# Low halves of two blocks moved to GpSimd, and the weight conversions placed one f later, in a gated linear attention and feed-forward kernel

## The chip, the cores and the metric

The kernel runs on one core of a Trainium2 chip. Its engines have instruction streams of their own: TensorE (PE in the profile; PEld is its weight load), VectorE (DVE), ScalarE (ACT), GpSimd (POOL) and SyncE (SP), which issues the transfers here. The metric is the device time of one execution in microseconds.

## What is computed

A gated linear attention over 4 batches, 8 heads, 768 steps and a head dimension of 48, whose output goes as 3072 tokens of 384 through a feed-forward layer of width 2048 with a leaky ReLU:

```python
for t in range(S):
    state = alpha[:, :, t, :, None] * state + np.einsum('bhd,bhe->bhde', k[:, :, t], v[:, :, t])
    y[:, :, t] = np.einsum('bhd,bhde->bhe', q[:, :, t], state)
x = y.transpose(0, 2, 1, 3).reshape(B * S, H * D)
h = x @ w_in
g = np.maximum(0.01 * h, h)
out = g @ w_out
```

q, k, v and alpha are float32. The two weight matrices are float64 and come to the kernel as pairs of 32-bit words.

## The kernel before

**Attention.** The work is cut into 24 units (a chunk of 128 tokens of one batch, all heads). The generator `attention` issues a unit in steps: `scans`, `scores`, `mask_scores` (a copy on ScalarE, L353, and a mask on GpSimd, L354), `k_tokens`, `scaled_q`, `scaled_k`, `outputs` (which writes x as a high half on ScalarE, L404, and a low half on VectorE, L405) and `next_state` (with a scaling on GpSimd, L359). Three units make a block `i` of 384 tokens, so there are eight blocks. Units 0 to 8 run first and give blocks 0, 1 and 2.

**Feed-forward.** An item is a pair (i, f): block i and one of 16 slices f of the width. `ffn_in` multiplies x by the weights of f. To keep precision, each operand is split into a high and a low half, and three products are summed: nine matmuls of 384 columns into one of two `ph` buffers (L473). Then L476 (ScalarE) makes `t` = 0.01 ph, L479 (VectorE) the maximum of it and ph, L481 (ScalarE) the high half `gh` and L485 (VectorE) the low half `gl`. `ffn_out` adds another nine matmuls (L498) per item into the output sums, `LAG` = 3 items later in program order. The items of blocks 0 and 1 alternate over f: (0,0), (1,0), (0,1), (1,1) and so on. The other blocks follow one by one, with the attention of the units 9 to 23 between their items. The first eight attention steps of that part are each held behind the low half (`made["gl", ...]`) of the item in front.

**Weights.** `load_weights(f)` brings slice f of both matrices into one of four `raw` buffers through SP's queue. When the last slice has been asked for, the loads of the units 9 and up follow behind it. `converting(f)` is a generator that turns the 64-bit words into a high and a low float32 half. It yields behind each of its eight steps: L233 (ScalarE, scales the upper words in place), L235 and L238 (VectorE, the float32 bits), L241 (ScalarE, the high half), L245 (VectorE, a power of two), L247 (VectorE, bits minus high half), L249 (VectorE, the lower words; the last reader of `raw`), L252 (VectorE, the low half).

**The order.** The framework's scheduler orders each engine's instructions, within edges that the kernel sets. `put(True, engine, op)` ties each instruction behind the last one that was put on the same engine's list, so that these lists are executed in program order:

```python
line = lines[eng]
with tc.issue_after(line[-1].ins) if line else nullcontext():
    line.append(op(*args))
```

`ffn_in` takes two tuples of generators and advances each one step per mention: the first tuple between L476 and L479, the second between L481 and L485. In the main loop `new` and `coming` are conversions on their way. Before the change, the conversions of f = 0 and f = 1 (`EARLY` = 2) are issued during the attention of the units 7 and 8, that of f = 2 as a whole behind x of unit 8, and from then on the conversion of f + 3 begins in item (0, f), while that of f + 2 is carried on and ends in the next f's first item. So one conversion overlaps the next, and is complete a whole f before its use. With the tuples of before, VectorE's list for one f reads L479, L235, L252, L238, L485 in item (0, f), and L245, L479, L247, L485, L249 in item (1, f), where L252 belongs to the older conversion.

Of the kernel before, what the change touches and what calls it, by code (L numbers as in the profile page):

```python
# [9 lines left out]
F32 = mybir.dt.float32  # L10
# [5 lines left out]
ALU = mybir.AluOpType  # L16
# [6 lines left out]
def gated_linear_attn_ffn(ctx, tc, q, k, v, alpha, w_in, w_out, out):  # L23
    nc = tc.nc
# [32 lines left out]
    PITCH = RUN + GAP  # L57
    AHEAD = 3 * UPB
    LAG = 3
    SOON, EARLY = 2, 2  # L60
    LEAD = 8
    SL = 8 * UPB

# [32 lines left out]
    def w_in_of(f, n, g):  # L96
        return w_sb[f][:, n, g * P:(g + 1) * P]
# [4 lines left out]
    made = {}  # L102
# [3 lines left out]
    def behind(*key):  # L106

        return tc.issue_after(made[key].ins) if key in made else nullcontext()
# [31 lines left out]
    def load_values(u):  # L140
        if u >= NU:
            return
        if u >= AHEAD and later is not None:
            later.append((load_values, u))
            return
        tb, b = units[u]
        made["v", u] = nc.sync.dma_start(
            vals_sb[u % NV].rearrange("t (h d) -> t h d", h=H),
            v[b, :, tb * C:(tb + 1) * C, :].rearrange("h t d -> t h d"),
        )  # L150
# [38 lines left out]
    def load_weights(f, part=None):  # L189

        if part != 1:
            jobs[f] = cvp.tile([P, 2 * NG, 2 * P], I32, name="raw", bufs=NRAW)
        raw = jobs[f]
        dst = raw.bitcast(I64) if f64 else raw[:, :, 0:P].bitcast(F32)
        for r, n, src, step, group in runs if part != 0 else ():
            a = w_in[src:src + n, f * P:(f + 1) * P]
            nc.sync.dma_start(  # L197
                dst[r:r + n, 0:NG], bass.AP(a.tensor, a.offset, [[step * DF, n], [group * DF, NG], list(a.ap[1])])
            )
        if part != 1:  # L200
            made["raw", f] = nc.sync.dma_start(dst[:, NG:], w_out[f * P:(f + 1) * P, :].rearrange("p (g f) -> p g f", g=NG))
# [3 lines left out]
    def put(ordered, eng, op, *args):  # L205

        if not ordered:
            return op(*args)
# [3 lines that stand above are left out]
        return line[-1]  # L212

    def converting(f, ordered=False):

        if f >= NF:
            return
        raw = jobs.pop(f)
        w_sb[f] = cst.tile([P, 2, 2 * DM], F32R, name=f"w{f}")
        hi, lo = w_sb[f][:, HIGH, :], w_sb[f][:, LOW, :]  # L220
        if not f64:
            val = raw[:, :, 0:P].bitcast(F32)
            hi, lo = (t.rearrange("p (g f) -> p g f", f=P) for t in (hi, lo))
            nc.scalar.copy(hi, val)
            made["w", f] = nc.vector.tensor_tensor(lo, val, hi.bitcast(F32), ALU.subtract)
            return
        words = raw.rearrange("p g (f w) -> p (g f) w", w=2)
        top, low = words[:, :, 1], words[:, :, 0]
        bits = cvp.tile([P, 2 * DM], I32, name="bits", bufs=NBITS)
        val = bits.bitcast(F32)  # L230

        with nullcontext() if lines["ACT"] else behind("hi", f - 1):
            put(ordered, "ACT", lambda: nc.scalar.mul(top.bitcast(F32), top.bitcast(F32), 2.0 ** -112))  # L233
        yield
        put(ordered, "DVE", lambda: nc.vector.tensor_scalar(  # L235
            bits, top, 3, 0x7FFFFFF8, ALU.logical_shift_left, ALU.bitwise_and))
        yield
        put(ordered, "DVE", lambda: nc.vector.scalar_tensor_tensor(  # L238
            bits, top, -0x80000000, bits, ALU.bitwise_and, ALU.bitwise_or))
        yield  # L240
        made["hi", f] = put(ordered, "ACT", lambda: nc.scalar.copy(hi, val))  # L241
        yield
        pw = cvp.tile([P, 2 * DM], I32, name="pw", bufs=NPW)
        rest = pw.bitcast(F32)
        put(ordered, "DVE", lambda: nc.vector.tensor_scalar(pw, bits, -0x800000, None, ALU.bitwise_and))  # L245
        yield
        put(ordered, "DVE", lambda: nc.vector.tensor_tensor(val, val, hi.bitcast(F32), ALU.subtract))  # L247
        yield
        put(ordered, "DVE", lambda: nc.vector.scalar_tensor_tensor(  # L249
            rest, low.bitcast(U32), 2.0 ** -52, rest, ALU.mult, ALU.mult))  # L250
        yield
        made["w", f] = put(ordered, "DVE", lambda: nc.vector.tensor_tensor(lo, rest, val, ALU.add))  # L252

    def convert(f):
        for _ in converting(f):
            pass
# [207 lines left out]
    def ffn_in(i, f, steps=None):  # L464

        ordered = steps is not None
        first, second = steps or ((), ())
        xh, xl = xs[i]
        ph = ps_h.tile([P, 512], F32, name="ph")[:, 0:TB]
        n = 0  # L470
        for g in range(NG):
            for wn, xt in ((HIGH, xh), (HIGH, xl), (LOW, xh)):
                nc.tensor.matmul(ph, w_in_of(f, wn, g), xt[:, g, :], start=n == 0, stop=n == 3 * NG - 1)  # L473
                n += 1
        t = ffp.tile([P, TB], F32, name="t")
        put(ordered, "ACT", lambda: nc.scalar.mul(t, ph, 0.01))  # L476
        for step in first:
            next(step, None)
        put(ordered, "DVE", lambda: nc.vector.tensor_tensor(t, ph, t, ALU.max))  # L479
        gh = ffp.tile([P, TB], F32R, name="gh", bufs=LAG + 1)  # L480
        put(ordered, "ACT", lambda: nc.scalar.copy(gh, t))  # L481
        for step in second:
            next(step, None)
        gl = ffp.tile([P, TB], F32R, name="gl", bufs=LAG + 1)
        made["gl", i, f] = put(ordered, "DVE", lambda: nc.vector.tensor_tensor(gl, t, gh.bitcast(F32), ALU.subtract))  # L485
        return gh, gl

    pos = {}
# [28 lines left out]
    gs = {}  # L517
# [8 lines left out]
    for n, _ in enumerate(st):  # L526
        if n == 2:
            load_values(NV - 1)
        while LOADS and LOADS[0][0] in made:
            key, f, part = LOADS.pop(0)  # L530
            with behind(*key):
                load_weights(f, part)
            loaded_f = f + 1
        u = AHEAD - EARLY + converted
        if converted < EARLY and ("ks", u) in made:
            with behind("ks", u):
                convert(converted)
            converted += 1
        if n in STARTS:
            i, f = items[len(gs)][:2]  # L540
            with behind(*STARTS[n]):
                gs[len(gs)] = ffn_in(i, f)
# [7 lines left out]
    new, coming = None, converting(EARLY + 1, True)  # L550
    next(coming)
    for n in range(len(items) + LAG):
        slices = 0
        if n < len(items):
            i, f, slices, _ = items[n]
            if f == 0:
                if i == 2:
                    st, held = attention(AHEAD, NU), 8
                while i not in ready:
                    next(st)  # L560
                emitted, due = 0, 0.0
            if loaded_f < NF:
                load_weights(loaded_f)
                loaded_f += 1
                if loaded_f == NF:
                    asked, later = later, None
                    with behind("raw", NF - 1):
                        for fn, *args in asked:
                            fn(*args)
            if n < len(STARTS):  # L570
                pass
            elif i == 0:
                old, new, coming = new or iter(()), coming, converting(f + SOON + 1, True)
                gs[n] = ffn_in(i, f, ((), (coming, new, old, new)))
            elif i == 1:
                gs[n] = ffn_in(i, f, ((new, new), (new,)))
                next(new, None)
            else:
                gs[n] = ffn_in(i, f)
        for half in range(2):  # L580
            due += slices / 2
            while emitted < due:

                with behind("gl", *items[n - 1][:2]) if held else nullcontext():
                    next(st, None)
                held = max(held - 1, 0)
                emitted += 1
            if half == 0 and n >= LAG:
                i, f, _, tag = items[n - LAG]
                ffn_out(i, f, gs.pop(n - LAG), tag)  # L590
# [129 lines left out]
```

## Time and the profile before

| what | value |
|---|---|
| median of 3 runs | 542.4 us (541.23 to 542.99) |
| profiled execution, first to last instruction (span) | 539.2 us |
| mean granted TensorE clock | 0.994 |
| L473, matmuls of `ffn_in` | 1152 of 338 ns mean |
| L479 and L485 on VectorE | 128 each of 550 ns mean |
| L476 and L481 on ScalarE | 128 each of 489 and 513 ns mean |
| a conversion's steps on VectorE (L235, L238, L245, L247, L249, L252) | 561, 950, 564, 969, 948, 970 ns mean |
| a conversion's steps on ScalarE (L233, L241) | 915, 838 ns mean |

The page names no total of the profiled execution but its span. Matmuls overlap, so their mean duration is longer than the distance from one to the next. Neighbouring VectorE instructions overlap too by some 0.08 us, so sums are made from starts and not from durations. In a row of the timeline stand start, duration, engine, line and operation, then what is written from what; in brackets the idle time in front of it and what ended it.

### The profile page before, as it was taken

The numbers are of one execution on the slowest core, as the hardware profiler recorded it, in microseconds if no ns is written. First come the engines' busy times: TensorE is split into PE (matmuls) and PEld (weight loads), VectorE is DVE, ScalarE is ACT, GpSimd is POOL, SyncE is SP. The second block draws the span as 40 slices with busy tenths as digits, with TensorE's granted clock in tenths as the row PEclk, the third lists the DMA queues.
The fourth block names the chain that finished last, engine by engine and source line by source line (L and its number), as shares of the span: only waits on it lengthen the run. The fifth ranks groups of instructions, "written<-read, shape, count | busy, mean of one in ns | idle before, by whom it ended". The sixth has DMA issues, their size and how long they took to land.

```text
span 539.2 us, 10037 instructions
## 1 busy us (share of the span) xinstructions
PE 522.2 (97%) x3778; PEld 501.8 (93%) x3778; DVE 380.5 (71%) x695; ACT 233.7 (43%) x494; POOL 60.2 (11%) x139
## 2 busy tenths in 40 slices
PE   8889889999999999999999999999999999999995
PEld 8778689999999899999999999999999999999995
DVE  6879999999998897875685775775876534333331
ACT  2755655555543543435334443344343344233332
POOL 4433500000000121110110101001100000000000
PEclk9999999999999999999999999999999999999999
DMA  9999954445723743533332422513301010101001
GB/s 146 166 182 181 198 136 117 118 122 139 190 49 86 197 104 83 106 77 97 75 80 59 119 49 63 104 43 98 70 1 39 1 44 1 23 1 44 1 0 50
DMA packets 92983, 46.64 MB, mean 87 GB/s; under 512 B 57856, under 2 KB 90112, under 8 KB 92928
## 3 DMA queue, kind: packets, MB, share of 16 engines
q1 hardware_dynamic: 92928, 45.93, 38.8%
q8 instruction: 32, 0.52, 0.5%
q14 instruction: 23, 0.19, 0.1%
HBM read 38.83 MB, written 4.72 MB: 81 GB/s over the span
## 4 chain that ended last, share of the span: by engine, by line
PE 87%; DMA 4%; DVE 3%; SPq 1%; issue 1%; ACT 1%; POOL 0%; ACTq 0%; DVEq 0%
PE ph L473 35%; PE b L498 32%; PE a L343 4%; PE a L498 4%; PE a L387 3%; DMA raw<-in_moe_w_in_dram 3%; PE a L381 2%; PE a L366 1%; PE a L398 1%; PE ph L160 1%; PE b L387 1%; PE b L267 1%; DMA small<-in_alpha_dram 1%; SPq L197 1%; DVE pc L301 1%
## 5 line engine op out<-in xcount | busy, mean ns | idle before, releaser
L473 PE MATMUL ph<-large,w 128*128 128x384 f32 x1152 | 226.0, 338 | 3.8 <-DVE t L479 3.8
L473 PEld LDWEIGHTS ph<-large,w 128*128 128x128 f32 x1152 | 200.6, 188 | 6.5 <-DVE t L479 4.8
L498 PE MATMUL b<-w,gh 128*128 128x384 f32 x672 | 169.4, 340 | 0.0
L479 DVE TENSOR_TENSOR t<-ph,t 128x384 f32<-128x384 f32 x128 | 70.4, 550 | 83.9 <-ACT t L476 83.6
L498 PEld LDWEIGHTS b<-w,gh 128*128 128x128 f32 x672 | 119.5, 188 | 2.1 <-ACT gh L481 0.4
L476 ACT ACTIVATE t<-ph 128x384 f32<-128x384 f32 x128 | 62.6, 489 | 135.1 <-PE ph L473 127.2
L481 ACT CAST gh<-t 128x384 fp32r<-128x384 f32 x128 | 65.7, 513 | 111.0 <-DVE t L479 108.6
L498 PE MATMUL b<-w,gl 128*128 128x384 f32 x336 | 107.3, 336 | 0.0
L485 DVE TENSOR_TENSOR gl<-t,gh 128x384 fp32r<-128x384 f32 x128 | 70.4, 550 | 33.4 <-ACT gh L481 29.7
L498 PEld LDWEIGHTS b<-w,gl 128*128 128x128 f32 x336 | 62.5, 188 | 0.1
L354 POOL TENSOR_SCALAR_AFFINE_SELECT sm<-sm 128x512 f32<-128x512 f32 x33 | 21.6, 665 | 121.4 <-ACT sm L353 103.8
L343 PE MATMUL a<-qs,ks 48*128 48x128 f32 x312 | 30.4, 286 | 0.0
L343 PEld LDWEIGHTS a<-qs,ks 48*128 48x128 f32 x312 | 25.4, 188 | 5.3 <-issue 4.7
L359 POOL TENSOR_TENSOR small<-us,pe 48x192 f32<-48x192 f32 x40 | 21.4, 536 | 79.1 <-DVE us L419 70.1
L276 DVE STREAM_TRANSPOSE ks<-small 128x512 f32<-128x512 f32 x15 | 16.7, 1122 | 13.4 <-PE a L366 13.4
L311 POOL COPY pe<-pc 128x4 f32<-128x4 f32 x24 | 5.0, 210 | 184.1 <-DVE pc L301 183.9
L353 ACT COPY sm<-a 128x512 f32<-128x512 f32 x24 | 14.0, 584 | 15.1 <-PE b L343 12.9
L301 DVE TENSOR_TENSOR_SCAN pc<-e,small 128x128 f32<-128x128 f32 x60 | 20.0, 394 | 0.0
L498 PE MATMUL a<-w,gh 128*128 128x384 f32 x96 | 19.7, 336 | 0.0
L307 DVE TENSOR_TENSOR_SCAN rc<-e,small 128x511 f32<-128x511 f32 x15 | 19.1, 1274 | 0.2
L387 PE MATMUL a<-sm,small 128*48 128x128 f32 x256 | 18.1, 278 | 0.3 <-POOL sm L354 0.3
L241 ACT CAST w<-bits 128x768 fp32r<-128x768 f32 x16 | 13.4, 838 | 11.1 <-DVE bits L238 11.0
(84 smaller groups left out, 552.6 us busy)
## 6 DMA issues: line engine op xcount, KB each, us to landing
raw<-in_moe_w_out_dram SPq DMA_DIRECT2D x16, 384.0 KB, 3.6
small<-in_v_dram SPq DMA_DIRECT2D x24, 192.0 KB, 3.9
raw<-in_moe_w_in_dram SPq DMA_DIRECT2D x32, 144.0 KB, 3.9
out_dram<-t SPq DMA_DIRECT2D x24, 192.0 KB, 1.9
small<-in_alpha_dram SPq DMA_DIRECT2D x32, 96.0 KB, 2.3
small<-in_q_dram SPq DMA_DIRECT2D x30, 96.0 KB, 2.4
small<-in_k_dram SPq DMA_DIRECT2D x30, 96.0 KB, 2.3
small<-in_alpha_dram SPq DMA_DIRECT2D x30, 80.0 KB, 2.3
```

Source lines behind the costliest of these rows:

```text
L301: nc.vector.tensor_tensor_scan(pc[:, p, :], aT[:, p, :], ones.broadcast_to([P, C]), 1.0, ALU.mult, ALU.mult)
L307: nc.vector.tensor_tensor_scan(flat[2][:, NP * C - 2::-1], flat[0][:, NP * C - 1:0:-1], flat[1][:, NP * C - 2::-1], last, ALU.mult, ALU.add)
L343: nc.tensor.matmul(ss[s][:, p, :], ks[lo:lo + D, p, :], qs[lo:lo + D, p, :], start=True, stop=True)
L354: nc.gpsimd.affine_select(out=sm[s], in_=sm[s], compare_op=ALU.is_ge, fill=0.0, base=0, pattern=[[0, NP], [1, C]], channel_multiplier=-1)
L359: nc.gpsimd.tensor_tensor(*scalings.pop(0))
L387: nc.tensor.matmul(y[lo:lo + m, p, :], V[:, c:c + m], masked[u][s][:, p, :], start=not tb and p == 0, stop=p == NP - 1, skip_group_check=True,
L473: nc.tensor.matmul(ph, w_in_of(f, wn, g), xt[:, g, :], start=n == 0, stop=n == 3 * NG - 1)
L476: put(ordered, "ACT", lambda: nc.scalar.mul(t, ph, 0.01))
L479: put(ordered, "DVE", lambda: nc.vector.tensor_tensor(t, ph, t, ALU.max))
L481: put(ordered, "ACT", lambda: nc.scalar.copy(gh, t))
L485: made["gl", i, f] = put(ordered, "DVE", lambda: nc.vector.tensor_tensor(gl, t, gh.bitcast(F32), ALU.subtract))
L498: nc.tensor.matmul(po[j], gt[:, js], w_out_of(f, wn), start=f == 0 and n == 0, stop=f == NF - 1 and n == 2)
```

## The change

The low half L485 of the items of blocks 0 and 1 is issued on GpSimd, outside of the ordered list. Only the conversion of f = 0 is left to the attention phase (`EARLY` = 1), still behind `ks` of unit 7; that of f = 1 is issued as a whole behind x of unit 8. From then on the conversion of f + 1 takes place inside f: L235 and L238 in front of L479 of item (0, f), L241, L245 and L247 behind L481 of it, L249 and L252 in front of L479 of item (1, f). Behind L481 of item (1, f) stands L233 of the conversion that follows.

```diff
-    SOON, EARLY = 2, 2
+    EARLY = 1
...
-        made["gl", i, f] = put(ordered, "DVE", lambda: nc.vector.tensor_tensor(gl, t, gh.bitcast(F32), ALU.subtract))
+        eng = nc.gpsimd if i < 2 else nc.vector
+        made["gl", i, f] = eng.tensor_tensor(gl, t, gh.bitcast(F32), ALU.subtract)
...
-        u = AHEAD - EARLY + converted
+        u = AHEAD - 1 - EARLY + converted
...
             elif i == 0:
-                old, new, coming = new or iter(()), coming, converting(f + SOON + 1, True)
-                gs[n] = ffn_in(i, f, ((), (coming, new, old, new)))
+                new, coming = coming, converting(f + EARLY + 1, True)
+                gs[n] = ffn_in(i, f, ((new, new), (new, new, new)))
             elif i == 1:
-                gs[n] = ffn_in(i, f, ((new, new), (new,)))
-                next(new, None)
+                gs[n] = ffn_in(i, f, ((new, new), (coming,)))
```

## The prediction

> **What bounds the kernel now.** First the page's busy times, then the stage that the change edits, in the windows: 80 to 158 us, where the pairs (0,f), (1,f) run and the weights of later f are converted.
>
> ```profile
> PE 522.2 (97%) x3778; PEld 501.8 (93%) x3778; DVE 380.5 (71%) x695; ACT 233.7 (43%) x494; POOL 60.2 (11%) x139
> 90.00:100.00 10.00, 10.00 (x60) 10.00 (x59) 10.00 (x17) 5.84 (x11) 0.00 (x0) 1.00 0.49 152
> ```
>
> In a window's row stand, after its length, the busy times of PE, PEld, DVE, ACT and POOL, then clock, DMA share and GB/s. TensorE and VectorE are both full in this stage, ScalarE half full, GpSimd empty. VectorE's share of 71% over the span says nothing of this. Which of the two sets the pace? The chain shows the turns of TensorE, the timeline those of VectorE:
>
> ```profile
> 94.58 1.56 PE a L498 x9
> 157.28 1.56 PE a L498 x9
> 499.23 3.13 PE b L498 x18
> 99.57 0.55 DVE L485 TENSOR_TENSOR gl<-t,gh 128x384 fp32r<-128x384 f32 x1
> 100.04 0.95 DVE L249 SCALAR_TENSOR_TENSOR pw<-raw,pw 128x768 f32<-128x768 uint32 x1
> 105.85 0.55 DVE L485 TENSOR_TENSOR gl<-t,gh 128x384 fp32r<-128x384 f32 x1
> ```
>
> Ten f take 157.28 - 94.58 = 62.7 us, 6.27 each. TensorE's 36 matmuls of one f at 3.13/18 = 0.174 us need 6.26. VectorE comes from one low half of such an item to the same one of the next f in 105.85 - 99.57 = 6.28 us, with ten instructions back to back (starts 0.47 apart behind a 384-wide one). So the two are balanced, and VectorE has no idle time because conversions of **two** f interleave: while one waits for ScalarE, the other has work. In this stage a lighter VectorE can gain next to nothing, as TensorE needs 6.26 anyway.
>
> **What the new order does.** Per f, VectorE loses two low halves (L485): 2 x 0.47 = 0.94, leaving 6.28 - 0.94 = 5.34 us. But `put` ties every ordered instruction behind the one before it on its engine, so the lists can be written down from the new tuples. VectorE: L235, L238, L479 of (0,f), L245, L247, L249, L252, L479 of (1,f). ScalarE: L476, L481 of (0,f), L241, L476, L481 of (1,f), L233 of the next conversion. Only one conversion is under way, and every step of it depends on the one in front through the two lists. A closed ring: L479 of (1,f), its L481, L233 (queued behind L481), L235, L238, L479 of (0,f+1) (queued behind L238), its L481, L241 (queued behind it), L247, L249, L252, and L479 of (1,f+1) behind that. It holds without TensorE. Its links can be read where the old kernel runs one conversion alone:
>
> ```profile
> 72.84 0.84 ACT L241 CAST w<-bits 128x768 fp32r<-128x768 f32 x1 [1.89 <-DVE bits L238]
> 73.71 0.96 DVE L247 TENSOR_TENSOR bits<-bits,w 128x768 f32<-128x768 f32 x1 [0.31 <-ACT w L241]
> 74.59 0.95 DVE L249 SCALAR_TENSOR_TENSOR pw<-raw,pw 128x768 f32<-128x768 uint32 x1
> 75.57 0.96 DVE L252 TENSOR_TENSOR w<-pw,bits 128x768 fp32r<-128x768 f32 x1
> 76.45 0.55 DVE L479 TENSOR_TENSOR t<-ph,t 128x384 f32<-128x384 f32 x1
> 76.92 0.55 DVE L235 TENSOR_SCALAR bits<-raw 128x768 int32<-128x768 int32 x1
> 77.09 0.52 ACT L481 CAST gh<-t 128x384 fp32r<-128x384 f32 x1 [2.23 <-DVE t L479]
> 77.50 0.96 DVE L238 SCALAR_TENSOR_TENSOR bits<-raw,bits 128x768 int32<-128x768 int32 x1
> 77.51 0.93 ACT L233 ACTIVATE raw<-raw 128x768 f32<-128x768 f32 x1
> 78.38 0.55 DVE L485 TENSOR_TENSOR gl<-t,gh 128x384 fp32r<-128x384 f32 x1
> ```
>
> Start to start: L479 to L481 0.64 (76.45, 77.09); L481 to ScalarE's next 0.42 (77.09, 77.51); L233 to L235 0.96 (its 0.93, and the 0.03 that lie between L241's end at 73.68 and L247); L235 to L238 0.58; L238 to VectorE's next 0.88 (77.50, 78.38). Then again 0.64 and 0.42; L241 to L247 0.87; L247 to L249 0.88; L249 to L252 0.98; L252 to L479 0.88. The sum is **8.15 us per f**, against 6.27. L245 is no link, it fits beside L481 and L241. VectorE is idle for 8.15 - 5.34 = 2.8 of it.
>
> **The low half on GpSimd.** The old trace has no such 128x384 instruction there. The nearest rows:
>
> ```profile
> L359 POOL TENSOR_TENSOR small<-us,pe x40: 502/507/1362, 16.6 to 387.2; 48x192 f32<-48x192 f32 x40
> L311 POOL COPY pe<-pc x24: 188/189/434, 7.6 to 415.2; 128x4 f32<-128x4 f32 x24
> L485 DVE TENSOR_TENSOR gl<-t,gh x128: 494/557/577, 68.2 to 530.9; 128x384 fp32r<-128x384 f32 x128
> ```
>
> The median of 192 elements is 0.51. Nothing per element gives 0.51 (VectorE's own 0.55 lies there), all per element 1.01. With L311's 0.19 as the fixed part, 384 elements cost 0.19 + 2 x 0.32 = 0.83, which I take. Does it hold up VectorE?
>
> ```profile
> 66.04 0.95 DVE L247 TENSOR_TENSOR bits<-bits,w 128x768 f32<-128x768 f32 x1
> 67.03 1.27 DVE L252 TENSOR_TENSOR w<-pw,bits 128x768 fp32r<-128x768 f32 x1
> 65.59 0.59 ACT L353 COPY sm<-a 128x512 f32<-128x512 f32 x1
> 66.24 1.24 POOL L354 TENSOR_SCALAR_AFFINE_SELECT sm<-sm 128x512 f32<-128x512 f32 x1 [1.53 <-ACT sm L353]
> L354 POOL TENSOR_SCALAR_AFFINE_SELECT sm<-sm x33: 631/637/1243, 12.4 to 451.0; 128x512 f32<-128x512 f32 x33
> ```
>
> GpSimd's mask came 0.06 after ScalarE ended (66.18), met L247 and took 1.24 instead of its median 0.64, to 67.48; L252, begun inside it, took 1.27 instead of 0.96 and ended 0.82 after it. They take turns, whole instructions at a time. So a low half starts 0.52 + 0.06 = 0.58 after its L481 began, ends at 1.41, and then holds up L247, due at 0.42 + 0.87 = 1.29, by 0.12, and L235, due at 0.42 + 0.96 = 1.38, by 0.03: **8.30 us per f**. At 0.51 it holds up nothing (8.15); at 1.01 it ends at 1.59 and costs 0.30 + 0.21 (8.66). The Trainium skill speaks against this part: in "GPSIMD Engine Reference", section "Performance versus the Vector engine", a two-input add of 2048 fp32 costs 1.96 times VectorE's time. On L485's 0.55 that makes an estimated 1.08, 8.80 per f and 577.2 us in all; no run so far shows it. Queued behind a low half on GpSimd are only masks and state scalings in the head, and nothing from 80 to 158 us.
>
> **The head.** Old: conversion 1 runs among unit 8's work, conversion 2 behind x of unit 8 (L405), and the next `ph` buffer comes late (timeline; the three short rows from 161.98 are the chain's):
>
> ```profile
> 64.03 0.84 ACT L241 CAST w<-bits 128x768 fp32r<-128x768 f32 x1
> 64.78 0.94 ACT L233 ACTIVATE raw<-raw 128x768 f32<-128x768 f32 x1
> 70.32 0.68 DVE L405 TENSOR_TENSOR large<-a,large 112x512 fp32r<-112x512 f32 x1
> 70.92 0.55 DVE L235 TENSOR_SCALAR bits<-raw 128x768 int32<-128x768 int32 x1
> 77.05 1.86 PE L473 MATMUL ph<-large,w 128*128 128x384 f32 x9 [1.97 <-DVE t L479]
> 161.98 1.58 PE ph L473 x9
> 163.63 0.50 ACT t L476
> 164.16 0.57 DVE t L479
> 160.08 1.38 PE L473 MATMUL ph<-large,w 128*128 128x384 f32 x7
> ```
>
> New: conversion 1 stands where conversion 2 stood, and conversion 2 runs inside f = 1. Without L241 and L233 in front of it, the mask copy of 65.59 starts some 1.6 earlier, so x of unit 8 comes at 70.3 - 1.6 = 68.7 (bounds 70.3, where that path doesn't carry, and 67.1, twice the gain, as five VectorE steps leave too). From there: L235 0.60, L238 0.58, L241 0.98, L247 0.87, L249 0.88, L252 0.98, ended 0.96 later: 74.5. The first item of f = 1 needs that low half from its third matmul on: 0.04 + 1.38, so 75.9. Then 0.07 + 0.53 to L479 (163.56 to 163.63 to 164.16): 76.5; 0.64 + 0.42 + 0.87 + 0.12 + 0.88 + 0.98 to the next L252, started 80.4, ended 81.4; the item (0,2) ends at 82.8. Old: 77.05 + 1.86 = 78.9. The head **loses 3.9 us** (2.3 to 5.5): one conversion fewer stands in front, but the remaining one comes later, and its successor is in line with the items.
>
> **The end of the stage.** Thirteen turns lie between (0,2) and (0,15): 82.8 + 13 x 8.30 = 190.7, where the old one ended at 160.08 + 1.38 = 161.46: 29.2 us late. Behind it TensorE is the bound and gives nothing back, but for one place:
>
> ```profile
> 170.00:180.00 10.00, 8.14 (x45) 7.50 (x44) 9.89 (x18) 3.09 (x8) 1.74 (x3) 1.00 0.70 179
> ```
>
> Here TensorE idles 1.86 us because block 3's attention begins on a full VectorE. Two of its eight held steps hang behind the low half of (1,15); that is now on GpSimd, so their VectorE part may go ahead. I take back half, 0.9 (0 to 1.86). Weight loads wait for a `raw` buffer until L249 has read it, so they and the attention loads queued behind them on SP come one f later plus the stage's delay; their first reader waits as long, so nothing.
>
> Sum: 3.9 + 25.3 (29.2 in all) - 0.9 = 28.3 us on the profiled execution. Its span is 539.2; the page has no other total for it, and the 3.2 us to the median of 542.4 I leave as they are: **570.7 us**. Lowest: 81.2 + 13 x 8.15 = 187.2, 25.7 - 1.9 = 23.8, 566.2. Highest: 84.4 + 13 x 8.66 = 197.0, 35.5, 577.9. Eleven links read to about 0.01, thirteen times, add 2 us on each side: 564 to 580.
>
> **Rivals.**
> *The lock alone* (0.08): the ring has slack that I don't see, and turns on the shared path set the pace. Conversion steps 6.28 - 4 x 0.47 = 4.40, two low halves 1.66, together 6.06, and with both L479 beside nothing 7.00. Against 6.27 that is 0 to 0.73 per f; with half of it and the head 542.4 + 3.9 + 4.7 = 551.
> *TensorE stays the bound, faster* (0.06): VectorE's 5.34 fits into 6.26, the head has one conversion less, and the stalls of 1.97 (77.05) and 1.86 go: 538.6. For it: VectorE is full everywhere. It decides if the ring's links shrink by a quarter, to 6.26; against it: they are starts measured with nothing between.
> *The same, but with the late head* (0.03): 3.9 lost, 3.8 regained: 542.5.
> *The clock* (0.03): TensorE at 6.26/8.30 = 75% may lose speed, as it did in the head:
>
> ```profile
> 30.00:40.00 10.00, 7.92 (x99) 6.73 (x99) 6.29 (x15) 5.49 (x15) 2.61 (x6) 0.91 0.96 167
> 40.00:45.00 5.00, 5.00 (x51) 4.69 (x47) 4.49 (x10) 3.06 (x7) 2.61 (x6) 0.84 1.24 196
> ```
>
> At half speed throughout, 12.5 per f: 13 x 6.2 = 81 more than before, 623. Against it: the 170 to 180 row, 81% busy at 1.00. "TensorE: Matmul & The Clock Gate" of the Trainium skill, section "HAM oscillation — how this bites in real kernels", puts the limit at idle gaps above some 3.4 us; the gaps here would be about 2.
>
> **Chances.** Forecast 0.80. Faster by over 0.3%: 0.06; within 0.3% (about what a measurement of this kernel tells from no change): 0.03; slower: 0.91. The range 564 to 580 is the forecast's own; what it leaves out are the rivals.
>
> **What would show it.** Right: per f 8.15 to 8.66 us between L252s; TensorE about 75% busy there, its idle time ended by L252; L235 idle behind L233 and L247 behind L241; GpSimd's low half near 0.83. Wrong: VectorE still full, or TensorE without gaps from 83 us on; a low half far above 1 us would make the turn longer than my upper bound; a halved clock would show in the windows.

## The result and the profile after

| | before | changed |
|---|---|---|
| median | 542.69 us (541.23 to 543.56, 4 runs) | 578.88 us (577.77 to 580.66, 4 runs) |
| ratio to before, 95% interval | | 1.0676 (1.0653 to 1.07) |
| span of the profiled execution | 539.2 us | 577.9 us |
| mean granted TensorE clock | 0.994 | 0.984 |

The changed kernel is slower by 36.2 us between the medians, and by 38.7 us between the two profiled spans. In the changed kernel's code the low half is line 486 and the output matmul line 499; the other lines named here keep their numbers.

The page's busy times and one window of the stage, in the order that the prediction explained:

```profile
PE 534.3 (92%) x3778; PEld 505.5 (87%) x3778; DVE 374.1 (65%) x663; ACT 232.2 (40%) x494; POOL 92.4 (16%) x171
90.00:140.00 50.00, 39.99 (x212) 36.45 (x213) 34.88 (x48) 19.99 (x36) 12.23 (x12) 1.00 0.36 95
```

Of 50 us, TensorE and VectorE were both busy for all of them before. Now VectorE is busy for 34.88, ScalarE for less than 20, GpSimd for 12, and still nothing is faster: no engine is full, so the time goes by what waits for what. One turn in the timeline, VectorE, ScalarE and GpSimd in order of time:

```profile
132.98 0.96 DVE L252 TENSOR_TENSOR w<-pw,bits 128x768 fp32r<-128x768 f32 x1
133.85 0.55 DVE L479 TENSOR_TENSOR t<-ph,t 128x384 f32<-128x384 f32 x1
134.51 0.51 ACT L481 CAST gh<-t 128x384 fp32r<-128x384 f32 x1 [3.23 <-DVE t L479]
134.93 0.91 ACT L233 ACTIVATE raw<-raw 128x768 f32<-128x768 f32 x1
135.10 1.02 POOL L486 TENSOR_TENSOR gl<-t,gh 128x384 fp32r<-128x384 f32 x1 [3.84 <-ACT gh L481]
135.88 0.66 DVE L235 TENSOR_SCALAR bits<-raw 128x768 int32<-128x768 int32 x1 [1.48 <-ACT raw L233]
136.57 0.96 DVE L238 SCALAR_TENSOR_TENSOR bits<-raw,bits 128x768 int32<-128x768 int32 x1
137.45 0.55 DVE L479 TENSOR_TENSOR t<-ph,t 128x384 f32<-128x384 f32 x1
138.16 0.51 ACT L481 CAST gh<-t 128x384 fp32r<-128x384 f32 x1 [1.95 <-PE a L499]
138.58 0.83 ACT L241 CAST w<-bits 128x768 fp32r<-128x768 f32 x1
138.75 1.02 POOL L486 TENSOR_TENSOR gl<-t,gh 128x384 fp32r<-128x384 f32 x1 [2.62 <-ACT gh L481]
139.44 1.15 DVE L247 TENSOR_TENSOR bits<-bits,w 128x768 f32<-128x768 f32 x1 [0.97 <-ACT w L241]
140.51 0.94 DVE L249 SCALAR_TENSOR_TENSOR pw<-raw,pw 128x768 f32<-128x768 uint32 x1
141.49 0.96 DVE L252 TENSOR_TENSOR w<-pw,bits 128x768 fp32r<-128x768 f32 x1
```

From L252 to L252 it takes 141.49 - 132.98 = 8.51 us. Every link begins within 0.2 us of the end of the one in front of it, on the other engine where the two differ: that is the ring. The low halves on GpSimd are no links of it. GpSimd's low half shows inside it as stretched instructions: L235, begun while a low half runs to 136.12, takes 0.66 instead of 0.55 and ends 0.42 after it; L247, begun while the next one runs to 139.77, takes 1.15 instead of 0.96 and ends 0.82 after it.

One turn is quite different. VectorE's timeline from 158 us on, with steps of the attention of unit 9 (L276, L301, L303, L302, L326, L307) among those of the conversion:

```profile
158.51 0.96 DVE L252 TENSOR_TENSOR w<-pw,bits 128x768 fp32r<-128x768 f32 x1
159.38 0.55 DVE L479 TENSOR_TENSOR t<-ph,t 128x384 f32<-128x384 f32 x1
161.41 0.66 DVE L235 TENSOR_SCALAR bits<-raw 128x768 int32<-128x768 int32 x1 [1.48 <-ACT raw L233]
163.84 1.08 DVE L276 STREAM_TRANSPOSE e<-small 128x512 f32<-128x512 f32 x1 [1.77 <-DMA small<-in_alpha_dram]
164.78 0.93 DVE L238 SCALAR_TENSOR_TENSOR bits<-raw,bits 128x768 int32<-128x768 int32 x1
165.64 0.53 DVE L479 TENSOR_TENSOR t<-ph,t 128x384 f32<-128x384 f32 x1
166.10 2.11 DVE L301 TENSOR_TENSOR_SCAN pc<-e,small 128x128 f32<-128x128 f32 x4
...
173.27 0.93 DVE L252 TENSOR_TENSOR w<-pw,bits 128x768 fp32r<-128x768 f32 x1
```

This turn takes 173.27 - 158.51 = 14.76 us. A transpose of alpha stands in front of L238 in VectorE's queue and waits 1.77 us for its transfer, and behind it the scans run in the middle of the ring.

Where the stage begins and ends, on VectorE and TensorE:

```profile
81.88 0.96 DVE L252 TENSOR_TENSOR w<-pw,bits 128x768 fp32r<-128x768 f32 x1
82.89 3.05 PE L473 MATMUL ph<-large,w 128*128 128x384 f32 x16 [1.56 <-DVE w L252]
199.31 0.96 DVE L252 TENSOR_TENSOR w<-pw,bits 128x768 fp32r<-128x768 f32 x1
200.32 3.04 PE L473 MATMUL ph<-large,w 128*128 128x384 f32 x16 [1.56 <-DVE w L252]
```

TensorE's first seven matmuls of such a row, 1.38 us as before, end item (0,2) at 84.3 and item (0,15) at 201.7. Before it was 78.9 and 161.46: 5.4 us late where the stage begins and 40.2 late where it ends. Of that, 1.5 come back by the end of the span.

### The profile page after: what moved, and what is told of

Its sections match the earlier page's. It is cut to its first block, busy times and chain, and to the rows that moved or that the text cites. A ratio compares the mean times of both kernels' runs of the same rounds, so it can differ in the third digit from the quotient of the medians.

```text
span 577.9 us, 10041 instructions
## 1 busy us (share of the span) xinstructions
PE 534.3 (92%) x3778; PEld 505.5 (87%) x3778; DVE 374.1 (65%) x663; ACT 232.2 (40%) x494; POOL 92.4 (16%) x171
## 4 chain that ended last, share of the span: by engine, by line
PE 78%; DVE 12%; ACT 4%; issue 2%; DMA 2%; SPq 1%; ACTq 0%; DVEq 0%
PE ph L473 34%; PE b L499 27%; PE a L343 4%; DVE bits L247 3%; PE a L387 3%; PE a L499 3%; PE a L381 2%; DVE pw L249 2%; DVE w L252 2%; ACT w L241 2%; ACT gh L481 1%; PE a L366 1%; PE a L398 1%; PE b L267 1%; DVE pc L301 1%
## 5 line engine op out<-in xcount | busy, mean ns | idle before, releaser
L473 PE MATMUL ph<-large,w 128*128 128x384 f32 x1152 | 229.1, 344 | 25.2 <-DVE w L252 24.5
L473 PEld LDWEIGHTS ph<-large,w 128*128 128x128 f32 x1152 | 203.7, 191 | 31.6 <-DVE w L252 29.2
L499 PE MATMUL b<-w,gh 128*128 128x384 f32 x672 | 171.6, 344 | 4.2 <-ACT gh L481 2.9
L479 DVE TENSOR_TENSOR t<-ph,t 128x384 f32<-128x384 f32 x128 | 70.2, 549 | 93.8 <-ACT t L476 93.6
L499 PEld LDWEIGHTS b<-w,gh 128*128 128x128 f32 x672 | 119.6, 189 | 10.5 <-ACT gh L481 8.6
L481 ACT CAST gh<-t 128x384 fp32r<-128x384 f32 x128 | 65.5, 513 | 151.4 <-DVE t L479 125.6
L476 ACT ACTIVATE t<-ph 128x384 f32<-128x384 f32 x128 | 62.4, 489 | 144.4 <-PE ph L473 138.6
L499 PE MATMUL b<-w,gl 128*128 128x384 f32 x336 | 107.5, 337 | 0.0
L486 DVE TENSOR_TENSOR gl<-t,gh 128x384 fp32r<-128x384 f32 x96 | 52.8, 550 | 31.9 <-ACT gh L481 31.9
L499 PEld LDWEIGHTS b<-w,gl 128*128 128x128 f32 x336 | 62.9, 189 | 0.3 <-issue 0.2
L486 POOL TENSOR_TENSOR gl<-t,gh 128x384 fp32r<-128x384 f32 x32 | 32.6, 1020 | 108.0 <-ACT gh L481 107.9
L359 POOL TENSOR_TENSOR small<-us,pe 48x192 f32<-48x192 f32 x40 | 23.3, 582 | 79.8 <-DVE us L419 71.0
L247 DVE TENSOR_TENSOR bits<-bits,w 128x768 f32<-128x768 f32 x16 | 17.9, 1121 | 13.4 <-ACT w L241 13.4
L276 DVE STREAM_TRANSPOSE ks<-small 128x512 f32<-128x512 f32 x15 | 16.8, 1121 | 13.5 <-PE a L366 13.5
L235 DVE TENSOR_SCALAR bits<-raw 128x768 int32<-128x768 int32 x16 | 10.4, 651 | 19.1 <-ACT raw L233 19.1
L301 DVE TENSOR_TENSOR_SCAN pc<-e,small 128x128 f32<-128x128 f32 x60 | 20.7, 405 | 0.0
L499 PE MATMUL a<-w,gh 128*128 128x384 f32 x96 | 20.3, 341 | 0.0
L307 DVE TENSOR_TENSOR_SCAN rc<-e,small 128x511 f32<-128x511 f32 x15 | 19.1, 1274 | 0.4
```

What stands on the lines that cost most here:

```text
L301: nc.vector.tensor_tensor_scan(pc[:, p, :], aT[:, p, :], ones.broadcast_to([P, C]), 1.0, ALU.mult, ALU.mult)
L307: nc.vector.tensor_tensor_scan(flat[2][:, NP * C - 2::-1], flat[0][:, NP * C - 1:0:-1], flat[1][:, NP * C - 2::-1], last, ALU.mult, ALU.add)
L359: nc.gpsimd.tensor_tensor(*scalings.pop(0))
L486: made["gl", i, f] = eng.tensor_tensor(gl, t, gh.bitcast(F32), ALU.subtract)
L499: nc.tensor.matmul(po[j], gt[:, js], w_out_of(f, wn), start=f == 0 and n == 0, stop=f == NF - 1 and n == 2)
```

## The experiments

All ratios are to the kernel before, run on the same chip in the same series. The theory: the ordered lists make a **ring**, and the rest is the taking of turns with GpSimd and the attention steps that got into the ring. The main rival: GpSimd's slow low half, by the turns that it takes, is the cause, and the order matters little.

**The order alone.** The changed kernel with the low half back on VectorE:

```diff
-        eng = nc.gpsimd if i < 2 else nc.vector
-        made["gl", i, f] = eng.tensor_tensor(gl, t, gh.bitcast(F32), ALU.subtract)
+        made["gl", i, f] = put(ordered, "DVE", lambda: nc.vector.tensor_tensor(gl, t, gh.bitcast(F32), ALU.subtract))
```

> The new order of the conversions, with the low half L485 of blocks 0 and 1 back on VectorE in the ordered list. Ring theory (one conversion at a time, every step behind the other engine's): the ring stays; L485 of (0,f) now stands between L247 and L249 and adds 0.46, so 8.15 + 0.46 = 8.61 us per turn; the attention steps of unit 9 are held on VectorE again, so there is no long turn of 14.8: 13 x 8.61 = 112 instead of 117.4 us, some 1.5 of it lost again at the start of the attention: about 575 us. Lock theory (GpSimd's low half in turn with VectorE's steps makes the stage slow): without it the turn falls to 7 us or less, below 556 us.

Measured: 576.38 us, ratio 1.0607 (1.0579 to 1.0635). Its first and its last turn:

```profile
82.08 0.96 DVE L252 TENSOR_TENSOR w<-pw,bits 128x768 fp32r<-128x768 f32 x1
193.53 0.96 DVE L252 TENSOR_TENSOR w<-pw,bits 128x768 fp32r<-128x768 f32 x1
```

Thirteen turns in 111.45 us, 8.57 each, none of them long. Without any low half on GpSimd most of the loss stays. The main rival falls.

**The engine alone.** The order of before, with L485 on GpSimd for blocks 0 and 1 (the hunk of the change at L485 and nothing else):

> The order of before, with only the low half of blocks 0 and 1 moved to GpSimd. Ring theory: two conversions overlap, so there is no ring; what is left is the taking of turns: VectorE 5.34 a turn plus two times 1.02 in which it waits, 7.4 us at most, 6.44 (4.40 + 2.04) at least, against 6.27: 542.7 + 13 x 0.2 to 13 x 1.1 = 545 to 557 us. If the low half on GpSimd were the main cause of the loss: 565 us or more. If it cost nothing: 541 to 543.

Measured: 554.31 us, ratio 1.0213 (1.0181 to 1.0246). VectorE in the middle of the stage, and GpSimd beside it (in this code, too, the low half is L486):

```profile
119.43 0.95 DVE L252 TENSOR_TENSOR w<-pw,bits 128x768 fp32r<-128x768 f32 x1
120.30 1.76 DVE L238 SCALAR_TENSOR_TENSOR bits<-raw,bits 128x768 int32<-128x768 int32 x1
123.90 1.78 DVE L249 SCALAR_TENSOR_TENSOR pw<-raw,pw 128x768 f32<-128x768 uint32 x1
126.53 0.95 DVE L252 TENSOR_TENSOR w<-pw,bits 128x768 fp32r<-128x768 f32 x1
```

```profile
119.67 1.57 POOL L486 TENSOR_TENSOR gl<-t,gh 128x384 fp32r<-128x384 f32 x1 [1.91 <-ACT gh L481]
123.80 1.07 POOL L486 TENSOR_TENSOR gl<-t,gh 128x384 fp32r<-128x384 f32 x1 [2.56 <-ACT gh L481]
```

A turn takes 7.10 us. VectorE saved two instructions of 0.47 and waits twice for GpSimd: L238 and L249 take 1.76 and 1.78 instead of 0.95. GpSimd waits too: 1.57 for an instruction of 1.02. An instruction that waits for the other engine is drawn as busy, so a full VectorE in this profile is partly a waiting one. This is what the rival "the lock alone" priced, at 551 us; on its own it costs a third of what the change cost. Two turns of this run are longer, 10.29 and 8.30 us (140.77 to 159.36), as the attention steps go ahead here too; they are gone where the steps are held (below).

**The held attention steps.** In the changed kernel the first of the eight held steps hang behind a low half that is on GpSimd, so nothing holds them on VectorE. Here they hang behind L479 instead:

```diff
-        put(ordered, "DVE", lambda: nc.vector.tensor_tensor(t, ph, t, ALU.max))
+        made["max", i, f] = put(ordered, "DVE", lambda: nc.vector.tensor_tensor(t, ph, t, ALU.max))
...
-                with behind("gl", *items[n - 1][:2]) if held else nullcontext():
+                with behind("gl" if items[n - 1][0] > 1 else "max", *items[n - 1][:2]) if held else nullcontext():
```

> The changed kernel, with the eight held attention steps behind L479 (VectorE) of the item in front where its low half is on GpSimd. Theory of the early steps: the turn of 14.8 us, in which VectorE waits for alpha of unit 9 and runs its scans, falls to 8.5, and with it the half clock of the turn of 9.2 (0.7); some 1.5 come back at the start of the attention: 578.9 - 6.2 - 0.7 + 1.5 = about 573.5 us. Rival (the long turn is the late transfer or the late weights, not the place of the steps): within 1 us of 578.9.

Measured: 574.16 us, ratio 1.0572 (1.0549 to 1.0596), which lies below the changed kernel's interval. The long turn is gone: in its trace the L252s of this part follow at 159.35, 167.88 and 176.42. The last one is at 193.48 instead of 199.31. The turn of 9.2, which was expected to go too, didn't: one of 9.21 stands elsewhere, from 98.94 to 108.15, after a stretch from 92 to 94 us in which TensorE's granted clock is 0.50.

**One link out of the ring.** L233 of the next conversion in front of L481 of (1,f) instead of behind it:

```diff
-                gs[n] = ffn_in(i, f, ((new, new), (coming,)))
+                gs[n] = ffn_in(i, f, ((coming, new, new), ()))
```

> The changed kernel, with L233 of the next conversion in front of L481 of (1,f) instead of behind it. Ring theory: L235 can follow L479 of (1,f) directly, so 0.64 + 0.42 + 0.96 + 0.13 leave the ring and 0.47 comes in: 8.51 - 1.68 = 6.8 by the lists alone; then the way through TensorE is the longer one (L252 ended 0.96, first item's matmuls 1.5, L476 and on to L479 0.6, then 0.71 + 0.42 + 1.06 + 0.98 + 0.88 over L481, L241, L247, L249 to L252): about 7.1 to 7.3 us a turn, 13 x 1.3 = 17 us less, about 562 us. Rival (the stage is bound by shared turns or by TensorE at a low clock, and not by the lists): no more than 3 us of difference.

Measured: 558.56 us, ratio 1.0301 (1.0268 to 1.0333). VectorE, with what ended its waits:

```profile
123.18 0.96 DVE L252 TENSOR_TENSOR w<-pw,bits 128x768 fp32r<-128x768 f32 x1
124.06 0.55 DVE L479 TENSOR_TENSOR t<-ph,t 128x384 f32<-128x384 f32 x1
124.52 0.55 DVE L235 TENSOR_SCALAR bits<-raw 128x768 int32<-128x768 int32 x1
125.11 0.96 DVE L238 SCALAR_TENSOR_TENSOR bits<-raw,bits 128x768 int32<-128x768 int32 x1
126.30 0.56 DVE L479 TENSOR_TENSOR t<-ph,t 128x384 f32<-128x384 f32 x1 [0.23 <-ACT t L476]
130.21 0.96 DVE L252 TENSOR_TENSOR w<-pw,bits 128x768 fp32r<-128x768 f32 x1
```

L235 follows L479 at once, the turn is 7.03 us, and L479 now waits for L476, that is, for TensorE: the longest way round has changed as expected. One instruction moved past one other is worth 20 us, 3 more than expected; the thirteen turns take 97.05 us instead of 117.43, and so hold the whole gain. This is the sharpest evidence for the ring: neither the amount of work on any engine nor the number of low halves on GpSimd has changed. What was the 14.8 us turn is in this run one of 10.56 (144.28 to 154.84) and one of 9.10 behind it, with the attention steps in them.

**Both of these.** L233 early, and the steps held behind L479:

> The changed kernel with L233 in front of L481 of (1,f), and with the eight held attention steps behind L479 of the item in front. Theory (the ring and the early attention steps are separate costs): the thirteen turns are all 7.03 us, 91.4 us instead of the 97.05 of the run with L233 moved alone, and about 1.5 come back at the start of the attention: 558.6 - 5.7 + 1.5 = about 554.5 us. If the two were one cost, seen twice: 558 us or more.

Measured: 555.21 us, ratio 1.023 (1.0192 to 1.0268). Thirteen turns from 80.83 to 172.28, 7.03 each: in the trace no long turn is left, and the regular ones are as before. The two costs are separate there. In the times the step from 1.0301 to 1.023 is small, and the two intervals touch.

**The engine alone, with the steps held.** The order of before, L485 on GpSimd, and the steps behind L479:

> The order of before with the low half of blocks 0 and 1 on GpSimd, as before, and now with the held attention steps behind L479 of the item in front. Theory: the two long turns of 10.3 and 8.3 us fall to 7.11, some 1.5 of the 4.4 come back at the start of the attention: 554.3 - 2.9 = 551.4 us, which leaves the price of the turns on the shared path alone. Rival (the long turns there are the weights' transfers): 554 within 1.

Measured: 552.47 us, ratio 1.0192 (1.0166 to 1.0217). From 84.67 us on, all turns in the trace are 7.11 us but the last, of 6.64. The direction is as expected, but the interval overlaps that of the run without the hold, so the 1.8 us between the two aren't shown. What stays is the price of taking turns: about 10 us, or turns of 7.11 us where they were 6.28 before.

**Toward a faster kernel.** The prediction named two stalls of the kernel before, 1.97 us at 77 us and 0.90 and 0.96 us between 174 and 181. The first: L479 of (0,1) queued behind the whole of conversion 2. Conversion 2 is opened around it:

```diff
-        for _ in converting(EARLY, True):
-            pass
+        started = converting(EARLY, True)
+        for _ in range(3):
+            next(started)
...
-    next(coming)
...
+                if f == 1:
+                    gs[n] = ffn_in(i, f, ((started,), (new, started, started), (started, started, coming, new, new)))
```

The third tuple is advanced behind the low half.

> The kernel before, with conversion 2 opened around the first item of f = 1: L479 of (0,1) stands in front of L245 of conversion 2, and its low half in front of L249. Theory (the stall of 1.97 at 77 us is L479 queued behind a whole conversion): TensorE fills it with the output matmuls of (0,1) and gains up to 1.9 us, of which some 1.2 can be kept, since in the kernel before the last low half of the weights is ready at 158.85 and its first reader starts at 160.08: 541.5 us. Rival (VectorE's full list sets the end of the stage, whatever its order in the head): 542.7 within 0.3.

Measured: 540.91 us over 12 runs, ratio **0.9974 (0.9958 to 0.999)**: below both kernels, by a little. TensorE (the output matmuls are L500 in this run's code):

```profile
75.62 1.21 PE L500 MATMUL b<-w,gh 128*128 128x384 f32 x6
76.67 0.69 PE L500 MATMUL b<-w,gl 128*128 128x384 f32 x3
77.54 1.50 PE L473 MATMUL ph<-large,w 128*128 128x384 f32 x7 [0.18 <-DVE w L252]
80.06 1.82 PE L473 MATMUL ph<-large,w 128*128 128x384 f32 x9 [1.02 <-DVE t L479]
```

The output matmuls fill the old stall, but 1.02 of it returns at 80 us, where L479 of (1,1) is late: as VectorE is full, part of the stall only moves. By the end of the stage nothing is left of the gain: the last L252 starts at 157.95, before it was 157.90, and the profiled execution spans 539.3 us against 539.2. The trace so goes with the rival, VectorE's full list, and the lower median isn't shown to come from the stall. All twelve runs were granted a clock of 0.994 or more, and the 14 of the 29 runs of the kernel before that had as much have a median of 541.2 us; why the clock was higher was not tried.

The second stall: the held steps are put behind the low half three items back instead of one (`items[n - 3]`).

> The kernel before, with the eight held attention steps behind the low half of the item three in front instead of one. Theory (the stalls of 0.90 and 0.96 us between 174 and 181 us come from the attention's start on a full VectorE, while it idles some 3 us between 159 and 166): the steps start some 5 us earlier, and up to 1.9 us is gained: 541 to 542 us. Rival (what VectorE gets earlier stands in front of L479 and L485 and only moves the stall): 542.5 to 545.

Measured: 541.95 us, ratio 0.9997 (0.9977 to 1.0018), no difference that can be told. The window of 170 to 180 us has TensorE busy for 9.96 instead of 8.14, but the one of 180 to 190 for 9.01 instead of 10.00, and the one of 160 to 170 for 9.83: most of the stall has moved. Both edits together:

> The kernel before with both edits, conversion 2 opened and the steps held three items back. If both theories hold, the gains add: 540 to 541 us. If VectorE's list sets the end of the stage and the stall only moves: 542 to 545.

Measured: 541.54 us, ratio 0.9986 (0.9972 to 1.0): between the two expectations. The interval overlaps those of both edits alone, so no gains that add are shown, and no worth of the second edit.

## Why the prediction was right, and where it was 8 us short

It said 570.7 us, and it is 578.88: 28.3 us of loss on record, 36.2 measured. The way in which the time is lost was right. That the time lies inside 564 to 580 is in part luck: the 6.5 us of the long turn (below) had no term in the range, and fit into width that had been left for other terms. By its own steps:

- **The balance of TensorE and VectorE and their interleaving** held. Without the second conversion under way VectorE's idle time came back, 15 us in 50.
- **The ring** held. Of the 8.51 us, contention and a buffer take 0.38 (below); the links alone make 8.13, where the sum on record had 8.15. The runs with the order alone and with L233 moved show that it is the cause.
- **The low half on GpSimd** was mis-sized. It takes 1.02 us, the upper bound of 1.01 (proportional to the elements), not 0.83 (a fixed part taken from L311). L247 to L249 became 1.07 instead of 0.88 and L235 to L238 0.70 instead of 0.58: 0.31 per turn where 0.15 was taken. With 1.01 the prediction would have taken 0.51 (8.66 per f), which is too much: a VectorE instruction begun inside a low half ends 0.82 (L247) and 0.42 (L235) after it, not a whole 0.96 and 0.55, as the 0.82 of its own mask row had shown. So two errors offset in part. The estimate by the Trainium skill's "GPSIMD Engine Reference" ("Performance versus the Vector engine"), 1.08, was nearer than mine; here the ratio to VectorE's 0.55 is 1.85 at 384 elements, not 1.96. Another 0.07 a turn had no term in the sum: L481 of (0,f) waits for output matmuls (its idle time ends by L499), probably the last readers of the `gh` buffer that it is to fill. Together nine regular turns are 0.21 longer than the 8.30 on record.
- **The end of the stage** is the step that failed: "their VectorE part may go ahead. I take back half, 0.9". The steps went ahead, but into the ring, where they cost a turn of 14.76 instead of 8.30, so 6.5 us. The prediction saw the hold move to GpSimd and asked only where the steps would no longer be late, not what stands behind them in VectorE's queue. The run with the hold shows it: 4.7 us less in all. What was to come back did, 1.5 us behind the stage, but at this price.
- **The head** lost 5.4 us instead of 3.9. The first low half of weights, forecast to end at 74.5, ended at 74.7, but the first item of f = 1 that waited for it took until 77.4 instead of 75.9, since TensorE ran at half clock then:

```profile
71.88 0.96 PE L473 MATMUL ph<-large,w 128*128 128x384 f32 x4 [0.75 <-ACT w L241]
74.74 4.18 PE L473 MATMUL ph<-large,w 128*128 128x384 f32 x14 [1.89 <-DVE w L252]
74.00:78.00 4.00, 3.26 (x10) 3.27 (x11) 2.15 (x4) 0.49 (x1) 0.00 (x0) 0.57 0.63 197
176.00:180.00 4.00, 4.00 (x14) 4.00 (x14) 2.97 (x5) 2.08 (x5) 1.39 (x2) 0.50 0.73 160
```

- **The rival of the clock** so came in for a small part: the half clock behind 74 us costs about 1.3, and the one behind the long turn leaves TensorE late, so that a turn after it takes 9.20 instead of 8.30 (its L481 waits for L499 and starts 1.41 behind L479 instead of 0.71). Through the regular turns, with gaps of about 1.6 us, the clock stayed at 1.00 in the 90 to 140 us row. That agrees with the limit of some 3.4 us in the Trainium skill's "TensorE: Matmul & The Clock Gate" ("HAM oscillation — how this bites in real kernels"). The slow window behind 74 us doesn't follow from it: the gaps in front of it are 0.75 and 1.89 us. Nor does that of 92 to 94 us in the run with the held steps: it stands behind a gap of 1.76 us. What sets the clock in this kernel stays open.

The sum on the spans: 5.4 (head) + 9 x (8.51 - 8.30) + 6.5 + 0.9 + 0.2 (the remaining turns) + 25.3 (on record for the thirteen) = 40.2 at the end of the stage; minus 1.5 makes the 38.7 measured.

## What to carry to other kernels

Where two engines hand a chain of steps to and fro in fixed lists, write the lists down and look for the closed ring; its length, not the busy time, is the least time of a turn, and a second chain in the lists can fill the waits. Taking work off a full engine gains nothing if the new order takes away the overlap that made it full. When an instruction that others are held behind moves to another engine, ask which queue they may now enter and what stands behind them there.

## What was not expected of the hardware

A 48x192 two-input instruction on GpSimd takes 0.507 us (median) and a 128x384 one 1.018: twice the elements per partition, twice the time, with no fixed part to be seen, although a copy of 4 elements takes 0.189.

In the run with the order alone, TensorE fell to half clock again and again, in windows of 3.4 us some 17 us apart:

```profile
100.70:104.10 3.40, 3.40 (x13) 3.40 (x12) 2.64 (x5) 1.80 (x4) 0.00 (x0) 0.52 0.70 210
104.10:117.80 13.70, 11.51 (x61) 10.38 (x61) 10.91 (x16) 4.90 (x9) 0.00 (x0) 0.99 0.26 64
117.80:121.20 3.40, 3.40 (x12) 3.40 (x12) 2.49 (x5) 1.84 (x3) 0.00 (x0) 0.51 0.74 209
```

The idle time of TensorE there is split into gaps of some 1.1 us and less, shorter than those of the changed kernel, whose clock stayed full over the same number of matmuls per turn. Why the shorter gaps drew the lower clock was not tried and stays open. It cost little: the turns are between 8.45 and 8.71 us, as the ring doesn't run through TensorE.
